# A fused attention and two-MoE kernel: a tile's value product moved in front of the next tile's scores

## Chip, cores, metric

The kernel runs on one core of one Trainium2 chip. The metric is the device time of one execution in microseconds (us). The times given are the median and the ends of several runs, and the rows below come from one more execution, taken by the hardware profiler.

## What is computed

Attention over pooled keys and values, then a dense feed-forward layer with an ELU, then a layer with eight experts, of which each token takes one. All is float32.

```python
def _attn_ref(q, k, v):            # q, k, v: (8, 8, 576, 64)
    k_p = k.reshape(B, H, 72, 8, D).mean(axis=3)
    v_p = v.reshape(B, H, 72, 8, D).mean(axis=3)
    attn = softmax(np.matmul(q, k_p.transpose(0, 1, 3, 2)) / np.sqrt(D))
    return np.matmul(attn, v_p)

x = attn_out.transpose(0, 2, 1, 3).reshape(4608, 512)
h = x @ w_in                       # (512, 2048)
g = np.where(h > 0, h, np.exp(np.minimum(h, 0)) - 1)
x = g @ w_out                      # (2048, 512)
logits = x @ w_gate                # (512, 8): one expert per token
for e in range(8):                 # w1: (512, 1024), w2: (1024, 512)
    out[mask] = gate_w[mask, None] * (np.maximum(x[mask] @ w1[e], 0) @ w2[e])
```

## The kernel before, in words

The 4608 tokens are 36 tiles of 128, and three tiles make one of 12 blocks (0 to 11). The dense layer runs in 192 steps: a step takes one block and one of the 16 slices of the 2048 hidden columns. Blocks 0 and 1 share steps 0 to 31 in quarters, and block `b` from 2 on has steps `16 b` to `16 b + 15`. In a step TensorE first makes the slice's hidden values (`g1_mm`, 12 products of 128x384, L506), ScalarE (ACT) and VectorE (DVE) apply the ELU to them (`elu_a` L516 to L518, `elu_b` L523 and L524, `elu_c` L530 and L531), and TensorE multiplies the values of two steps ago with `w_out` (`g2`, 9 products of 128x512, L548). float32 products are split into three products of rounded parts (`xh`, `xl` and so on).

The attention of a block is spread over the steps of the block in front of it, and the routing of a block over the steps of the block behind it. Which operation lies in which step is written out by hand: `at(n, slot, fn, ...)` puts `fn` into a slot of step `n`, and `step(n)` runs the slots in a fixed order. `pe_mid` lies between `g1_mm` and `g2` on TensorE, `dve_pre` in front of the ELU, `act_mid` behind `elu_b`, `end` at the end of the step. Each engine works through its own queue in that order, and so do the DMA queues of SP and of POOL (GpSimd).

For a tile `t` from 9 on: `s_mm` (L410) makes the scores of 8 heads on quarters of the array, into two PSUM banks; `s_max`, `s_exp` and `s_norm` make probabilities of them, `q_turn` (L446) turns these on VectorE in blocks of 32, and `q_move` (L454) copies the pieces into `aT`, half of the copies on ACT and half on VectorE, in two parts. `pv_mm` (L479) multiplies `aT` with the values, and `pv_copy` (L492, L493) writes the result as `xh` and `xl`, the input of the dense layer. If the scores are in step `n`, the turn is at the end of `n + 1`, the two moves are in `n + 2` and `n + 3`, and the value product is in `n + 4`. The scores of the three tiles of a block lie in steps 0, 5 and 10 of the block in front of it. The turned pieces, `aT` and the wide tile of probabilities (`s_wide`) have one buffer each, and scores, value products and counts go round three PSUM banks.

With the scores go, at a fixed distance: the load of q (`a_load`, on SP), eight transfers that sum up k and v of a batch (`k_link`, `v_link`; the first on SP, seven accumulating ones on POOL), and the scaling of k (`k_scale`). The routing of a block has 24 logits on VectorE (L599), then `r_top`, `r_weight`, and `r_count` (L662, L663), which counts the tokens' places with two small products; `r_put` works the places out on VectorE and scatters them to the list `tab` with three transfers on POOL. The last 16 steps (block 11) and all behind them belong to the experts.

Of the kernel before, what the change touches and what calls it, by code (L numbers as in the profile page):

```python
# [25 lines left out]
NT = NTOK // P  # L26
TB = 3
NBLK = NT // TB
BT = TB * P
DFF = 2048  # L30
NF = DFF // P
# [24 lines left out]
T_TURN = 9  # L56
# [41 lines left out]
def fused_kernel(ctx: ExitStack, tc: tile.TileContext, q, k, v, w_in, w_out, w_gate, w1, w2, cst, out):  # L98
# [595 lines left out]
    def at(n, slot, fn, *args):  # L694
        events.setdefault((n, slot), []).append((fn, args))
# [3 lines left out]
    def score_at(t, n, slot="pe_mid"):  # L699
        at(n, slot, s_mm, t)  # L700
        n += slot == "pe_end"
        for hh in range(2):
            at(n, "dve_pre", s_max, t, hh)
        at(n, "act_mid", s_exp, t, 0)
        n += t not in (7, 8)
        at(n, "act_mid", s_exp, t, 1)
        at(n, "dve_mid" if t in SCORE0 else "end", s_norm, t)

    def turn_at(t, n):
        at(n + 1, "end", q_turn, t)  # L710
        for part in range(2):
            at(n + 2 + part, "act_mid", q_move, t, part)
        at(n + 4, "pe_mid", pv_mm, t)
        at(n + 4, "act_mid", pv_copy, t)

    def trans_at(t, n):
        at(n, "pe_end" if t in OUT else "pe_mid", t_mm, t)
        for hh in range(2):
            at(n, "act_end" if t in OUT else "act_mid", t_copy, t, hh, nc.scalar.copy)
        out = OUT.get(t, ((n, "pe_end"), (n + 1, "pre")))  # L720
        at(*out[0], pv_mm, t)
        at(*out[1], pv_copy, t)

    at(2 * NF - 1, "end", s_wide)
    first_of = {b: b * S // P for b in range(B)}
    SCORE = {6: (20, "pe_mid"), 7: (24, "pe_mid"), 8: (28, "pe_mid")}
    TRANS = {6: 23, 7: 26, 8: 30}
# [5 lines left out]
    for t in range(2 * TB, NT):  # L733
        if t not in SCORE:
            blk, j = divmod(t, TB)
            SCORE[t] = (NF * (blk - 1) + 5 * j, "pe_mid")
            at(SCORE[t][0] - 6, "end", a_load, t)
        else:
            at(SCORE[t][0] - 6, "end", a_load, t)
        score_at(t, *SCORE[t])  # L740
        if t >= T_TURN:
            turn_at(t, SCORE[t][0])
        else:
            trans_at(t, TRANS[t])
    for b in range(2, B):
        n0 = SCORE[first_of[b]][0]
        for j in range(POOLW):
            at(n0 - 22 + j, "end", k_link, b, j)
            at(n0 - 14 + j, "end", v_link, b, j)
        at(n0 - 2, "end", k_scale, b)  # L750
# [35 lines left out]
    for x, (w, c) in enumerate(chunks):  # L786
        n = 2 + x
# [16 lines left out]
    def route_at(blk, n0, per):  # L804
        at(n0 - 3, "end", r_gate_load, blk, 0)
        at(n0 - 2, "end", r_gate_load, blk, 1)
        at(n0 - 1, "end", r_gate_load, blk, 2)
        n = 0
        for x in range(NE * TB):
            e, j = divmod(x, TB)  # L810
            at(n0 + n, ("dve_mid", "end", "end", "end")[x - sum(per[:n])], r_logit, blk, e, j)
            if j == TB - 1 and e + 3 < NE:
                at(n0 + n, "end", r_gate_load, blk, e + 3)
            if x + 1 == sum(per[:n + 1]):
                n += 1
        n += n0
        at(n, "dve_mid", r_top, blk)
        at(n + 1, "dve_mid", r_weight, blk)
        if blk < last - 1:
            at(n + 2, "pe_mid", r_count, blk)  # L820
            at(n + 2, "end", r_put, blk)

    route_at(1, 30, [1, 2, 2, 2, 2, 3, 3, 3, 3, 3])
    route_at(0, 41, [2, 2] + [3] * 6 + [2])
    route_at(2, 3 * NF + LAG + 1, [2, 2, 2, 2, 3, 3, 3, 3, 4])
    for blk in range(3, last):
        route_at(blk, NF * (blk + 1) + LAG, [3, 2, 3, 2, 3, 2, 3, 2, 2, 2])
# [572 lines left out]
    for k in range(1, len(main)):  # L1400
        kind, prev = main[k][0], main[k - 1][0]
        for u in range(TILES[kind]):
            if kind == "T":
                n = 4 * k - 2
            elif prev == "T":
                n = 4 * k - TILES[kind] + u
            else:
                n = 4 * k - 1
# [170 lines left out]
```

## Time and profile before

| what | value |
|---|---|
| median of 3 runs | 1442.6 us (1439.48 to 1446.41) |
| the profiled execution | 1439.03 us |
| its span, first to last instruction | 1437.2 us |
| TensorE (PE) busy | 1379.6 us, 96% of the span |
| VectorE (DVE) busy | 988.5 us, 69% |
| ScalarE (ACT) busy | 773.4 us, 54% |
| GpSimd (POOL) busy | 199.3 us, 14% |
| TensorE's granted clock, mean | 0.983 of full speed |

Times in the rows are counted from the first instruction. A tile's name is the program's, with the buffer's number left out; `out<-in` says what an instruction writes and reads. Steps 32 to 175 run from 189.13 to 902.97 us of the span. The releaser that the profile names for a wait is inferred from the time at which semaphores changed; where two engines ended nearly together it can be the other one.

### The profile page before, as it was taken

The numbers are of one execution on the slowest core, as the hardware profiler recorded it, in microseconds if no ns is written. First come the engines' busy times: TensorE is split into PE (matmuls) and PEld (weight loads), VectorE is DVE, ScalarE is ACT, GpSimd is POOL, SyncE is SP. The second block draws the span as 40 slices with busy tenths as digits, with TensorE's granted clock in tenths as the row PEclk, the third lists the DMA queues.
The fourth block names the chain that finished last, engine by engine and source line by source line (L and its number), as shares of the span: only waits on it lengthen the run. The fifth ranks groups of instructions, "written<-read, shape, count | busy, mean of one in ns | idle before, by whom it ended". The sixth has DMA issues, their size and how long they took to land. (4 is left out here: it accounts for less than half of the span.)

```text
span 1437.2 us, 23781 instructions
## 1 busy us (share of the span) xinstructions
PE 1379.6 (96%) x8481; PEld 1176.2 (82%) x8482; DVE 988.5 (69%) x2395; ACT 773.4 (54%) x1889; POOL 199.3 (14%) x208
## 2 busy tenths in 40 slices
PE   8999999999999999999999999999999999999996
PEld 5798888878888888888888888998888888778785
DVE  7899878887777868686868778795646544335261
ACT  6777756565666656666656566462333233334251
POOL 0011011111111211110210000020212122112020
PEclk9999999999999999999999999999999999999999
DMA  9166435556333372554461331356476447758460
GB/s 341 59 183 196 115 83 88 68 70 93 56 69 64 70 74 57 65 78 62 87 79 41 60 34 51 60 166 128 154 113 174 132 148 244 253 190 312 148 227 22
DMA packets 109144, 169.43 MB, mean 118 GB/s; under 512 B 15509, under 2 KB 53015, under 8 KB 109016
## 3 DMA queue, kind: packets, MB, share of 16 engines
q1 hardware_dynamic: 91528, 135.45, 38.6%
q0 software_dynamic: 17488, 32.37, 10.8%
q8 instruction: 69, 1.13, 0.4%
q14 instruction: 59, 0.48, 0.2%
HBM read 146.35 MB, written 21.88 MB: 117 GB/s over the span
## 5 line engine op out<-in xcount | busy, mean ns | idle before, releaser
L548 PE MATMUL y<-woh,gh 128*128 128x512 f32 x576 | 238.2, 414 | 2.0 <-DVE yr L562 2.0
L548 PE MATMUL y<-wol,gh 128*128 128x512 f32 x576 | 232.2, 403 | 0.0
L548 PE MATMUL y<-woh,gl 128*128 128x512 f32 x576 | 231.2, 401 | 0.0
L599 DVE SCALAR_TENSOR_TENSOR junk<-yr,wgb 128x512 bf16<-128x512 f32 x264 | 180.8, 685 | 4.4 <-ACT yr L564 1.3
L523 DVE SCALAR_TENSOR_TENSOR g<-g,th 128x384 f32<-128x384 f32 x192 | 106.4, 554 | 101.7 <-ACT th L518 101.0
L530 ACT CAST gh<-g 128x384 fp32r<-128x384 f32 x192 | 98.8, 515 | 136.0 <-DVE g L524 86.9
L506 PE MATMUL h<-xh,wih 128*128 128x384 f32 x768 | 168.3, 340 | 1.5 <-ACT xh L492 1.5
L506 PE MATMUL h<-xl,wih 128*128 128x384 f32 x768 | 166.5, 338 | 0.0
L506 PE MATMUL h<-xh,wil 128*128 128x384 f32 x768 | 165.9, 337 | 0.0
L516 ACT ACTIVATE th<-h 128x384 f32<-128x384 f32 x192 | 94.0, 490 | 131.8 <-PE h L506 131.7
L1222 DVE SCALAR_TENSOR_TENSOR hlD<-mhD,hhD 128x512 fp32r<-128x512 f32 x64 | 44.2, 691 | 161.3 <-ACT hhD L1221 155.9
L506 PEld LDWEIGHTS h<-xh,wih 128*128 128x128 f32 x768 | 139.7, 190 | 18.1 <-ACT xh L492 2.0
L1221 ACT ACTIVATE hhD<-mhD 128x512 fp32r<-128x512 f32 x64 | 38.4, 601 | 199.2 <-PE myD L1244 191.6
L531 DVE TENSOR_TENSOR gl<-g,gh 128x384 fp32r<-128x384 f32 x192 | 106.9, 557 | 44.9 <-ACT gh L530 39.2
L506 PEld LDWEIGHTS h<-xh,wil 128*128 128x128 f32 x768 | 137.7, 188 | 0.0
L506 PEld LDWEIGHTS h<-xl,wih 128*128 128x128 f32 x768 | 137.4, 188 | 0.2
L548 PEld LDWEIGHTS y<-woh,gh 128*128 128x128 f32 x576 | 111.2, 193 | 27.6 <-issue 7.2
L548 PEld LDWEIGHTS y<-woh,gl 128*128 128x128 f32 x576 | 111.8, 194 | 25.6
L548 PEld LDWEIGHTS y<-wol,gh 128*128 128x128 f32 x576 | 111.6, 194 | 17.5
L524 DVE TENSOR_TENSOR g<-g,h 128x384 f32<-128x384 f32 x192 | 106.3, 554 | 6.6
L518 ACT ACTIVATE th<-th 128x384 f32<-128x384 f32 x192 | 100.8, 525 | 6.2
L517 ACT ACTIVATE g<-th 128x384 f32<-128x384 f32 x192 | 100.8, 525 | 6.2
(282 smaller groups left out, 2350.3 us busy)
## 6 DMA issues: line engine op xcount, KB each, us to landing
wgb<-in_moe_w_gate_dram SPq DMA_DIRECT2D x96, 256.0 KB, 4.5
w1stD<-in_moe_w_dram SPq DMA_DIRECT2D x32, 512.0 KB, 4.4
w2stD<-in_moe_w_dram SPq DMA_DIRECT2D x32, 512.0 KB, 4.6
qT<-in_q_dram SPq DMA_DIRECT2D x36, 256.0 KB, 8.8
ybuf<-yr SPq DMA_DIRECT2D x33, 256.5 KB, 7.6
raw<-in_moe_w_in_dram SPq DMA_DIRECT2D x16, 512.0 KB, 7.6
raw<-in_moe_w_out_dram SPq DMA_DIRECT2D x15, 512.0 KB, 6.2
t1U<-in_moe_w_dram SPq DMA_DIRECT2D x12, 512.0 KB, 8.5
```

Source lines behind the costliest of these rows:

```text
L506: mark["g1"] = nc.tensor.matmul(ps, wi[i][a][:, c, o:o + P], bb[blk][:, c, :], start=n == 0, stop=n == 3 * KC - 1).ins
L516: nc.scalar.activation(th, hps[blk, f], AF.Relu, scale=-1.0)
L517: nc.scalar.activation(g, th, AF.Exp, scale=-1.0)
L518: nc.scalar.activation(th, th, AF.Tanh, scale=-0.5)
L523: nc.vector.scalar_tensor_tensor(g, g, 1.0, th, op0=ALU.add, op1=ALU.mult)
L524: nc.vector.tensor_max(g, g, hps.pop((blk, f)))
L530: nc.scalar.copy(gh, g)
L531: nc.vector.tensor_sub(gl, g, gh)
L548: nc.tensor.matmul(ys[blk][j], a[:, js], wo[i][bb][:, o, :], start=n == 0 and f in FIRST[blk], stop=n == 2 and f in LAST[blk],)
L599: nc.vector.scalar_tensor_tensor(junk, yrows[blk][j][:, :DM], 1.0, pes[blk, e], op0=ALU.mult, op1=ALU.mult, accum_out=lgs[blk][:, j, e:e + 1])
L1221: nc.scalar.activation(hh, ps, AF.Relu)
L1222: nc.vector.scalar_tensor_tensor(hl, ps, 0.0, hh, op0=ALU.max, op1=ALU.subtract)
```

## The change

The value product and its copy are taken out of `turn_at` (four steps behind the scores) and put into the step of the next tile's scores, registered in front of these; for tile 35 they stay in step 174. The scores of block 4 and later blocks lie in steps -2, 3 and 8 instead of 0, 5 and 10 of the block in front; those of tiles 9, 10 and 11 lie in steps 31, 36 and 41 instead of 32, 37 and 42. `s_wide` is made at the end of step 30 instead of 31. `r_count` and `r_put` of blocks 0 to 9 lie three steps behind `r_top` instead of two. No operation is added or left out.

```diff
@@ def turn_at(t, n)
         for part in range(2):
             at(n + 2 + part, "act_mid", q_move, t, part)
-        at(n + 4, "pe_mid", pv_mm, t)
-        at(n + 4, "act_mid", pv_copy, t)
@@
-    at(2 * NF - 1, "end", s_wide)
+    at(2 * NF - 2, "end", s_wide)
@@ for t in range(2 * TB, NT)
             blk, j = divmod(t, TB)
-            SCORE[t] = (NF * (blk - 1) + 5 * j, "pe_mid")
+            SCORE[t] = (NF * (blk - 1) + 5 * j - 2 if blk > 3 else 2 * NF - 1 + 5 * j, "pe_mid")
+            if t > T_TURN:
+                at(SCORE[t][0], "pe_mid", pv_mm, t - 1)
+                at(SCORE[t][0], "act_mid", pv_copy, t - 1)
             at(SCORE[t][0] - 6, "end", a_load, t)
@@
             trans_at(t, TRANS[t])
+    at(NF * (NBLK - 1) - 2, "pe_mid", pv_mm, NT - 1)
+    at(NF * (NBLK - 1) - 2, "act_mid", pv_copy, NT - 1)
@@ def route_at(blk, n0, per)
         if blk < last - 1:
-            at(n + 2, "pe_mid", r_count, blk)
-            at(n + 2, "end", r_put, blk)
+            at(n + 3, "pe_mid", r_count, blk)
+            at(n + 3, "end", r_put, blk)
```

## Rows read from the trace of the kernel before

**Rows 1.** Page, part 1: busy us (share of the span) and instructions of each engine.
```profile
PE 1379.6 (96%) x8481; PEld 1176.2 (82%) x8482; DVE 988.5 (69%) x2395; ACT 773.4 (54%) x1889; POOL 199.3 (14%) x208
```

**Rows 2.** TensorE's waits and their releasers: us in total, times, longest us.
```profile
PE pv L479 <- ACT th L516: 30.5, 22, 2.8
PE pv L479 <- DVE aT L454: 5.9, 5, 2.0
PE y L548 <- DVE yr L562: 2.0, 1, 2.0
PE pos L663 <- DVE acc L652: 1.6, 8, 0.2
```

**Rows 3.** Timeline, steps 115 and 116: start, length, engine, line, operation [idle before].
```profile
607.88 0.55 DVE L523 SCALAR_TENSOR_TENSOR g<-g,th 128x384 f32<-128x384 f32 x1
...
609.05 0.93 DVE L454 COPY aT<-turned 32x256 f32<-32x256 f32 x3
...
609.52 0.48 ACT L516 ACTIVATE th<-h 128x384 f32<-128x384 f32 x1
...
610.12 1.09 PE L479 MATMUL pv<-aT,v 72*64 72x128 f32 x16 [1.26 <-ACT th L516]
...
611.15 0.50 PE L548 MATMUL y<-woh,gh 128*128 128x512 f32 x1
```

**Rows 4.** Timeline, step 41.
```profile
237.33 1.09 PE L479 MATMUL pv<-aT,v 72*64 72x128 f32 x16 [1.83 <-DVE aT L454]
...
238.40 0.48 ACT L516 ACTIVATE th<-h 128x384 f32<-128x384 f32 x1
```

**Rows 5.** Windows, 27 steps with value product: length, busy us per engine, PEclk, DMA.
```profile
206.66:215.77 9.11, 7.03 (x38) 5.75 (x37) 8.66 (x24) 5.22 (x12) 0.44 (x1) 0.81 0.34 76
...
866.06:872.50 6.44, 5.48 (x39) 4.64 (x37) 6.25 (x19) 4.27 (x9) 0.00 (x0) 1.00 0.14 43
890.07:898.79 8.72, 7.12 (x40) 5.84 (x39) 6.11 (x21) 5.09 (x12) 0.00 (x0) 0.80 0.41 98
sum 202.12, PE 163.74 PEld 136.36 DVE 176.04 ACT 121.74 POOL 22.23; mean PE 6.06 PEld 5.05 DVE 6.52 ACT 4.51 POOL 0.82
```

**Rows 6.** Windows, sums over 27 steps with scores, then 90 with neither.
```profile
sum 136.10, PE 136.10 PEld 116.89 DVE 110.12 ACT 82.52 POOL 11.29; mean PE 5.04 PEld 4.33 DVE 4.08 ACT 3.06 POOL 0.42
...
sum 375.62, PE 375.62 PEld 341.28 DVE 272.17 ACT 238.47 POOL 55.70; mean PE 4.17 PEld 3.79 DVE 3.02 ACT 2.65 POOL 0.62
```

**Rows 7.** Windows of steps 29 and 31, a value product without a wait.
```profile
173.31:178.69 5.38, 5.38 (x40) 4.56 (x38) 3.45 (x8) 3.58 (x14) 0.00 (x0) 1.00 0.05 14
183.62:189.13 5.51, 5.51 (x41) 4.70 (x38) 3.07 (x8) 3.52 (x8) 1.70 (x3) 1.00 0.22 30
```

**Rows 8.** Timeline of TensorE in the prologue.
```profile
22.07 1.10 PE L479 MATMUL pv<-aT,v 72*64 72x128 f32 x16
23.09 0.73 PE L410 MATMUL sp<-kT,qT 64*64 64x72 f32 x32
23.75 1.09 PE L479 MATMUL pv<-aT,v 72*64 72x128 f32 x16
```

**Rows 9.** Windows of steps 42 and 78: counts behind scores, behind a value product.
```profile
240.53:245.63 5.10, 5.10 (x56) 4.38 (x55) 4.83 (x21) 2.10 (x5) 0.00 (x0) 1.00 0.63 145
...
419.59:426.95 7.36, 5.75 (x41) 4.75 (x39) 6.01 (x21) 5.10 (x12) 0.00 (x0) 1.00 0.17 61
```

**Rows 10.** Windows of blocks 2, 3 and 7: length, busy us of PE, PEld, DVE, ACT, POOL.
```profile
189.13:271.26 82.13, 76.24 (x484) 66.94 (x482) 70.01 (x193) 48.38 (x134) 11.67 (x13) 0.96 0.48 71
271.26:353.75 82.49, 76.70 (x501) 67.33 (x500) 67.74 (x198) 49.47 (x137) 10.49 (x12) 0.96 0.58 81
...
589.08:666.54 77.46, 73.56 (x484) 64.92 (x482) 60.12 (x163) 49.29 (x136) 11.61 (x13) 1.00 0.50 70
```

**Rows 11.** Timeline: ELU of step 119, first product of step 121.
```profile
628.76 0.55 DVE L524 TENSOR_TENSOR g<-g,h 128x384 f32<-128x384 f32 x1
...
630.89 0.87 PE L506 MATMUL h<-xh,wih 128*128 128x384 f32 x4
```

**Rows 12.** Window from step 176 to the end.
```profile
902.97:1437.20 534.23, 522.41 (x2759) 432.32 (x2757) 270.63 (x572) 193.99 (x301) 94.57 (x88) 0.99 0.56 166
```

## The prediction

> **What bounds the kernel now.** I read the page's engine line first: TensorE is busy in 1379.6 of 1437.2 us [rows 1], so 57.6 us of the span are TensorE idle time, and no other engine is near its limit as a whole. What can be won is idle time of TensorE, or busy time in which it runs slowly. The list of TensorE's waits says where the idle time lies: in front of the value product `pv` of a tile there are 30.5 + 5.9 us, and the next entry is a single wait of 2.0 [rows 2].
>
> The timeline of one such step shows what the wait is for [rows 3]. TensorE ends the first product of step 116 and stands still for 1.26 us, until `pv` starts at 610.12. The list names ACT's `th` (it ends at 610.00) as the releaser, but `pv` does not read `th`. It reads `aT`, and VectorE's last copy into `aT` (L454) ends at 609.98. In step 41 the two can be told apart: there `pv` starts behind the copy, and `th` only starts 1.07 us after `pv` has [rows 4]. So it is a wait for the move of the turned probabilities. That copy is late for a plain reason: in VectorE's queue it stands behind the two ELU operations of its step (L523 at 607.88), which need ACT's `tanh` of a product that TensorE ended a step earlier. With the value product four steps behind the scores, TensorE gets there 1 to 2 us too soon every time.
>
> The windows over whole steps give the size. The 27 steps with a value product take 202.12 us, TensorE is busy in 163.74 of them, so 38.4 are idle. Nine of the 27 show a granted clock of 0.80 to 0.84 instead of 1.00, the first and the last of them in the rows [rows 5]: the clock fell to its lower level (1.2 instead of 2.4 GHz) behind the pause. These two last 9.11 and 8.72 us, a step with a short pause and no fall 6.44. The 27 steps with scores take 136.10 us with no idle time, and the 90 steps with neither take 375.62, which is 4.174 each [rows 6]. Together, steps 32 to 175 are 713.84 us.
>
> **The change part by part.** *Value product.* Of tiles 9 to 34 it moves to the step of the next tile's scores, directly in front of them: five steps behind its own scores (six between blocks) instead of four. Tile 35 stays six behind. The copies gain a plain step of 4.17 us and were late by 1 to 2. So some 2 to 3 us are left over in an ordinary block, the wait should go, and with it the pauses behind which the clock fell. A value product without a wait is in the trace twice, in steps of 5.38 and 5.51 us [rows 7]: 1.21 and 1.34 over a plain step. I take 1.28.
>
> *The pair.* Scores alone cost 136.10 / 27 - 4.174 = 0.87 [rows 6]. Side by side they cost less: in the prologue, scores start 1.02 us behind the start of a value product, and the next value product 0.66 behind the scores, with no pause [rows 8]. The full-array product also starts 1.03 behind a value product (610.12 to 611.15 in [rows 3]), so scores put between the two add 0.66, not 0.87. A pair: 1.28 + 0.66 = 1.94.
> The Trainium skill's page "TensorEngine Tiling (Array Packing)", section Tiling Modes, says that a change of the tiling mode drains TensorE; `pv` (72*64) and the scores (64*64) are different tilings, so by that page the pair would still pay a drain in its middle. Estimated at half of the 0.21 that lone scores pay for two changes, this would be 2.04 for a pair, 2.6 us more for 26 of them. The prologue's rows show no such extra between the two, so they decide.
>
> *Scores* move two steps sooner (tiles 9 to 11: one), and with them the loads of q (SP), the links of k and v (the first on SP, seven accumulating transfers on POOL), the scaling of k (VectorE) and the strip of zeros (POOL). I cost these at nothing: they keep their distance to the scores, no wait for q or k is in the list, whose largest entries stand in [rows 2], and the buffers that they refill are released sooner by as many steps. If that cover were gone, a late q or k would stop TensorE for as long as it is late, once per tile or batch.
>
> *Counts.* The two small products of `r_count` move one step on. Today they cost 0.06 where they lie behind scores (5.10 against the mean of 5.04), and 0.30 of busy time where they lie behind a value product (5.75 - 4.174 - 1.28), with a wait for `acc` of 0.2 on top [rows 2, 9]. A step later `acc` is long done. I take 0.3 for each of ten. Their scatters (three on POOL each) come a step later, in front of links that have 14 steps in hand. VectorE's five short operations behind the counts now follow the norm and turn of the next block's first tile. The lists still read `acc` two steps after the last of them.
>
> *What is late next: VectorE.* Its work does not shrink, while TensorE's time does. At the new prices a block takes 16 x 4.174 + 3 x 1.94 + 0.3 = 72.9 us. VectorE is busy 60.1 in an ordinary block, but 70.0 in block 2 and 67.7 in block 3, where earlier blocks are routed as well [rows 10]. In an ordinary block 12.8 us are left; its tightest place is the first product that reuses the bank which the ELU reads: it starts 1.58 us behind the ELU (629.31 to 630.89) [rows 11], and by the order of the queues I find about that much after the change. In blocks 2 and 3 VectorE would have to work 96% and 93% of the time, though each tile's scores hold it up. There TensorE will have to wait for VectorE: for a bank, or for the copy of y (one wait of 2.0 us in [rows 2]; the second half of a move now lies in that copy's step). The trace of before does not show how long. From below it is 0. From above, blocks 2 and 3 keep the 82.1 and 82.5 us that they have, which gives back 19 us. I take 5, nearer the low end, since most of the 12 and 15 us that VectorE idles in them today comes with TensorE's own pauses.
>
> *The sum.* Steps 32 to 175 after: 144 x 4.174 = 601.0; 26 pairs 50.4; the value product of tile 35 1.3; the scores of tile 9, which now join a value product in step 31, 0.7; ten counts 3.0; VectorE 5.0. That is 661.4, so 52.4 less than 713.8. Behind step 175 TensorE is busy in 522.4 of 534.2 us [rows 12] and does the same as now, only sooner. The profiled execution took 1439.03 us (its span of 1437.2 and 1.8 around it): 1439.03 - 52.4 = 1386.6, say 1387. The median of the three runs is 3.6 above that execution. I don't add this: two or three more clock falls are as much, and the falls should go. It stays in the range.
>
> **The rivals.**
> *VectorE bounds the routing blocks.* 19 us instead of 5: 1401. For it: 70.0 of 72.9. Against: it is only two blocks, and the bank has 1.58 in hand. Chance 0.10.
> *The clock still falls.* If the chip takes two small products in a row, 1.9 us on a part of the array, as it takes a pause, the clock falls in a third of the pairs, as now in nine of 27. A fall costs about 1.4 us (8.72 against 7.36 for steps with the same work [rows 5, 9]), nine of them some 13: 1400. Against it: in step 169 a pause of 0.96 and a value product of 1.09, two microseconds with less work than a pair has, left the clock at 1.00 [rows 5]. Chance 0.08.
> *The wait moves along.* The value product waits for something that comes later, too, say a bank of the same step, and the pauses stay: about 1439. That in step 41 it starts right behind the copy speaks against it. Chance 0.02.
> *Slower.* TensorE works in order, so a value product that waits now holds up the scores behind it. Their maxima stand in VectorE's queue in front of the ELU and of the next copies, so lateness feeds on itself. To end above 1446, each of 26 pairs would need a wait of (52 + 7) / 26 = 2.3 us, that is copies about 5 us later against TensorE's steps than today. That needs VectorE without spare time in ordinary blocks, and it has 12.8 us. It would be some 1450. Chance 0.03.
>
> **How the numbers follow.** The forecast has 0.77, and 1376 to 1396 is its own range: no loss to VectorE and shorter pairs at the low end, 10 us of loss, a drain per pair and the 3.6 of the median at the high end. The range that should hold the time 8 times in 10 goes on to the first two rivals: 1374 to 1403. About 0.5%, 7 us, is what a measurement of this kernel can tell from no change. Faster by more: the forecast and the first two rivals, 0.95; the same 0.02; slower 0.03.
>
> **What would show it.** Right: no `pv` wait of tens of us in TensorE's list; `pv` and `sp` back to back, with starts 1.0 apart; steps with a pair of about 6.1 us; no or nearly no clock falls between 200 and 850 us; ordinary blocks of about 73 us. New in the list would be waits of `h` or `y` for VectorE, in blocks 2 and 3 above all, some 5 us together. Wrong: `pv` still waits behind the last copy; `sp` starts more than 1.2 behind `pv`; clock falls inside pairs; or ordinary blocks that keep 77 us, with waits for VectorE in them.

## The result and the profile after

| | before | after |
|---|---|---|
| median | 1442.07 us (1439.48 to 1446.41, 4 runs) | 1384.34 us (1382.43 to 1385.67, 4 runs) |
| ratio | | 0.9606, 95% interval 0.9582 to 0.9629 |
| profiled execution | 1439.03 us, span 1437.2 | 1385.67 us, span 1383.8 |
| steps 32 to 175 | 713.84 us | 659.89 us |
| from step 176 on | 534.2 us | 534.6 us |

The kernel is 57.7 us faster by the medians and 53.4 by the profiled executions; in these all of it lies in steps 32 to 175. The engine line of the page answers to [rows 1]: TensorE is idle for 26 us of the span where it was for 58.

```profile
PE 1357.7 (98%) x8481; PEld 1164.8 (84%) x8482; DVE 983.7 (71%) x2395; ACT 772.1 (56%) x1889; POOL 199.2 (14%) x208
```

The list of TensorE's waits (us in total, times, longest us) answers to [rows 2]. No tile from 9 on waits for its value product any more, and the counts don't wait. The first line is the old wait in step 22. The others are new; they name the copies of y's rows or, with `part`, the addition of block 0's parts to them.

```profile
PE y L548 <- DVE yr L562: 2.3, 1, 2.3
PE y L548 <- ACT yr L564: 1.6, 1, 1.6
...
PE y L548 <- DVE part L588: 1.4, 1, 1.4
...
PE y L548 <- DVE yr L566: 1.2, 1, 1.2
```

The timeline of steps 114 and 115 is the counterpart of [rows 3] for the first tile of an ordinary block (tile 24). VectorE's last copy into `aT` ends at 569.78, the value product starts at 574.25, 4.5 us later and without a pause. The scores of the next tile start 1.02 behind it, the full-array product 0.67 behind these, as in the prologue of the kernel before [rows 8].

```profile
568.89 0.89 DVE L454 COPY aT<-turned 32x256 f32<-32x256 f32 x3
...
574.25 1.09 PE L479 MATMUL pv<-aT,v 72*64 72x128 f32 x16
...
575.27 0.73 PE L410 MATMUL sp<-kT,qT 64*64 64x72 f32 x32
...
575.94 0.50 PE L548 MATMUL y<-woh,gh 128*128 128x512 f32 x1
```

The windows answer to [rows 5, 6, 9]: the sum over the 26 steps with a pair (a value product directly in front of the next tile's scores), over the ten steps with counts, and over the 107 steps with neither; then steps 34, 50 and 174 (the value product of tile 35), one by one (length, busy us of each engine, PEclk, DMA).

```profile
sum 158.93, PE 158.93 PEld 136.28 DVE 139.13 ACT 95.56 POOL 19.24; mean PE 6.11 PEld 5.24 DVE 5.35 ACT 3.68 POOL 0.74
...
sum 43.50, PE 43.50 PEld 37.92 DVE 20.69 ACT 26.82 POOL 0.83; mean PE 4.35 PEld 3.79 DVE 2.07 ACT 2.68 POOL 0.08
...
sum 452.07, PE 447.94 PEld 405.41 DVE 388.98 ACT 315.59 POOL 68.36; mean PE 4.19 PEld 3.79 DVE 3.64 ACT 2.95 POOL 0.64
...
197.69:203.48 5.79, 4.43 (x22) 3.75 (x21) 5.66 (x15) 4.06 (x10) 1.73 (x2) 1.00 0.23 31
271.99:280.03 8.04, 5.27 (x22) 4.06 (x22) 7.81 (x23) 6.08 (x13) 0.00 (x0) 0.92 0.55 38
839.50:844.89 5.39, 5.39 (x38) 4.58 (x37) 4.26 (x17) 2.56 (x6) 0.00 (x0) 1.00 0.67 148
```

Busy time equals length in the steps with pairs and counts. The 4.1 us by which 452.07 exceeds 447.94 are TensorE's only idle time between steps 32 and 175: 1.36 in step 34 and 2.77 in step 50. Behind the second the clock falls, once; step 51, a pair of 7.05 us, carries the rest of it. Blocks 2, 3 and 7 answer to [rows 10]:

```profile
189.31:263.61 74.30, 72.94 (x483) 64.88 (x482) 68.01 (x189) 47.51 (x134) 11.75 (x13) 1.00 0.51 89
263.61:341.47 77.86, 75.09 (x501) 66.06 (x500) 68.29 (x197) 50.34 (x143) 9.23 (x9) 0.98 0.55 72
559.56:632.29 72.73, 72.73 (x484) 64.86 (x483) 59.84 (x163) 49.21 (x137) 9.02 (x10) 1.00 0.50 71
```

The ordinary block is TensorE's work and nothing else. Blocks 2 and 3 keep 1.6 and 5.1 us more than it.

### The profile page after: what moved, and what is told of

Its sections match the earlier page's. It is cut to its first block, busy times and chain, and to the rows that moved or that the text cites. A ratio compares the mean times of both kernels' runs of the same rounds, so it can differ in the third digit from the quotient of the medians.

```text
span 1383.8 us, 23759 instructions
## 1 busy us (share of the span) xinstructions
PE 1357.7 (98%) x8481; PEld 1164.8 (84%) x8482; DVE 983.7 (71%) x2395; ACT 772.1 (56%) x1889; POOL 199.2 (14%) x208
## 4 chain that ended last, share of the span: by engine, by line
PE 85%; DVE 5%; issue 5%; ACT 3%; DMA 1%; POOL 0%; SPq 0%; POOLq 0%; ACTq 0%; DVEq 0%
PE h L506 25%; PE y L548 25%; PE mhD L1212 13%; PE myD L1247 13%; PE pv L479 2%; PE sp L410 1%; PE zTD L1142 1%; DVE dec L227 1%; DVE dec L231 1%; ACT gh L530 1%; DVE junk L599 1%; PE mhT L1212 1%; ACT dec L220 1%; PE vsum L345 1%; DVE dec L225 1%
## 5 line engine op out<-in xcount | busy, mean ns | idle before, releaser
L548 PE MATMUL y<-woh,gh 128*128 128x512 f32 x576 | 230.6, 400 | 6.4 <-DVE yr L562 2.3
L548 PE MATMUL y<-wol,gh 128*128 128x512 f32 x576 | 226.6, 393 | 0.0
L548 PE MATMUL y<-woh,gl 128*128 128x512 f32 x576 | 226.5, 393 | 0.0
L1224 ACT ACTIVATE hhD<-mhD 128x512 fp32r<-128x512 f32 x64 | 38.4, 601 | 199.3 <-PE myD L1247 183.9
L548 PEld LDWEIGHTS y<-woh,gh 128*128 128x128 f32 x576 | 108.1, 188 | 28.0 <-issue 2.8
L548 PEld LDWEIGHTS y<-woh,gl 128*128 128x128 f32 x576 | 108.3, 188 | 24.0
L548 PEld LDWEIGHTS y<-wol,gh 128*128 128x128 f32 x576 | 108.3, 188 | 16.2
```

Source lines behind the costliest of these rows:

```text
L548: nc.tensor.matmul(ys[blk][j], a[:, js], wo[i][bb][:, o, :], start=n == 0 and f in FIRST[blk], stop=n == 2 and f in LAST[blk],)
```

## The experiments

Three questions: is the wait of the value product really one for the copies into `aT`; which part of the change carries how much; and is VectorE what holds up blocks 2 and 3 now. The theory is that of the prediction. Its rivals were that `pv` waits for ACT's `th`, that the sooner scores and not the later value product bring the gain, and that pairs or the place of the counts are worth nothing.

**e1: value products four steps behind their scores again, all else changed.**

```diff
-                at(SCORE[t][0], "pe_mid", pv_mm, t - 1)
+        at(n + 4, "pe_mid", pv_mm, t)      # in turn_at; pv_copy alike
```


> The changed kernel with one part undone: the value product of tiles 9 to 35 is four steps behind its own scores again, in a step of its own; scores stay sooner, counts stay later. Theory (the gain is the wait for the move of aT, and the clock falls behind it): the waits come back, TensorE's list shows some 27 waits of pv of 1 to 2 us, 25 to 40 us in all, clock falls come back (3 to 12 of them), pairs are gone; 1425 to 1445 us. Rival (the gain comes from VectorE's work lying better once the scores are sooner): at most 1395 us, with few pv waits.

1407.5 us (1403.6 to 1409.1; ratio to before 0.9746, 0.9715 to 0.9776). Neither had it: the later value product (with the pairs) brings 23 of the 58 us, sooner scores and later counts together bring 35. How these 35 divide was not run on its own; e9 below shows the counts alone to be worth 2 us or nothing. TensorE's waits for the value product, by who ended them:

```profile
PE pv L479 <- ACT th L516: 12.1, 9, 1.8
PE pv L479 <- DVE aT L454: 4.9, 11, 0.9
```

The windows of steps 114, 119 and 124 (first, second and third tile of a block; columns as above):

```profile
583.23:588.62 5.39, 5.39 (x39) 4.58 (x37) 4.18 (x10) 4.56 (x10) 0.00 (x0) 1.00 0.04 3
606.14:612.64 6.50, 5.47 (x38) 4.62 (x37) 6.31 (x19) 4.28 (x10) 0.62 (x1) 1.00 0.59 109
630.22:635.93 5.71, 5.48 (x39) 4.63 (x37) 5.55 (x15) 3.56 (x8) 0.87 (x1) 1.00 0.24 36
```

Waits come back, but 17 us in all instead of 38, and three clock falls instead of nine. So it matters which steps of a block the moves lie in. The first tile's are now in steps 0 and 1, which have no logits, instead of 2 and 3, which have three and two, and four steps are enough (no idle time, 1.26 us before). The second tile's lie among two or three logits as before, and it waits 1.03 us (0.96 before). The third tile's left steps 12 and 13, and its wait falls from 1.4 to 0.23 us. That is not a matter of logits: those two steps have none, but `r_top` and `r_weight`. In the first of them ACT stood 2.58 us until VectorE had made `lg`, and what ACT had queued behind that came late, as this line of the kernel before shows (step 124, for the value product of step 126):

```profile
654.25 0.22 ACT L627 ACTIVATE lg<-lg 128x24 f32<-128x24 f32 x1 [2.58 <-DVE lg L626]
```

Which of the operations in front of the moves costs how much, no run separates.

**e3 and e8: the kernel before, with the moves in front of the ELU instead of behind it; e8 also has the counts one step later.**

```diff
-            at(n + 2 + part, "act_mid", q_move, t, part)
+            at(n + 2 + part, "dve_pre", q_move, t, part)
 # e8 also:
-            at(n + 2, "pe_mid", r_count, blk)          # r_put alike
+            at(n + 3, "pe_mid", r_count, blk)
```


> The kernel before with one edit: the moves into aT stand in front of the ELU of their step (slot dve_pre) instead of behind it; the value product stays four steps behind the scores. Theory (pv waits for VectorE's last copy, which stands behind the ELU): the pv waits fall from 36 us to under 5, the clock falls with them from nine to at most two, 1385 to 1400 us. Rival (pv waits for ACT's th, the releaser that the list names): th moves no sooner, the pv waits stay at 30 us or more, 1435 to 1446 us.

e3 takes 1450.7 us (1448.0 to 1454.2; ratio 1.006, 1.004 to 1.008): 0.6% slower, above the ranges of both. But the waits of `pv` fell, from 36.4 us to 12.1 (not to under 5: the first tile of a block still waits 1.2 us), so they do follow the copies. The time was lost in other waits, of TensorE for the counts above all, and of the hidden-value products `h` for the ELU, which now stands behind the copies:

```profile
PE pos L662 <- DVE roh L650: 22.2, 10, 2.5
PE pv L479 <- ACT th L518: 9.3, 8, 1.2
PE h L506 <- DVE g L524: 5.7, 10, 3.0
...
PE pv L479 <- DVE aT L454: 2.3, 5, 0.9
```

The counts of step 14 need `roh`, which VectorE makes behind the ELU of the step in front; the wait of `pv` had covered that. With that cover gone the pause moves from in front of the value product to behind it, gets longer (2.5 instead of 1.4 us), and the clock still falls behind it. e8 moves the counts away from there:

> The kernel before with the moves in front of the ELU (as in e3) and the counts one step later: that step no longer has a value product, so that a late r_weight stops nothing. Theory (pv waits for the copies; in e3 the time was lost again at the counts): waits of pos for roh gone, pv waits about 11 us as in e3, few clock falls; 1400 to 1415 us, some 30 us under the kernel before. Rival (moves in front of the ELU cost as much as they save, whatever the counts do): 1435 us or more.

1408.1 us (1407.7 to 1409.0; ratio 0.9771, 0.9736 to 0.9806), as the theory had it. The waits of `pv` are 13.0 us, and no clock fall is left between steps 32 and 175: its list of waits, then the window over these steps:

```profile
PE pv L479 <- ACT th L518: 9.4, 8, 1.2
PE h L506 <- DVE g L524: 3.4, 10, 1.1
PE pv L479 <- DVE aT L454: 3.0, 6, 1.3
...
188.44:870.79 682.35, 663.35 (x4389) 582.04 (x4388) 556.26 (x1515) 444.48 (x1223) 87.76 (x96) 1.00 0.45 70
```

So the order of one kind of copies and the place of two small products are worth 33 us together, with scores and value products where they were. That `pv` waits for the copies is shown; the releaser in the list was an accident of two ends lying together. The trace of the kernel before also shows for which half of them: in 24 of its 27 steps `pv` starts 0.10 to 0.25 us behind the end of VectorE's last copy, while ACT's last copy had ended 0.98 to 2.45 us before that start. (The other three tiles span two batches; there `pv` starts 0.2 us before VectorE's last copy ends.) ACT's last copies for the value product of [rows 3] end at 607.87, 2.25 us before it starts:

```profile
606.64 1.23 ACT L454 COPY aT<-turned 32x256 f32<-32x256 f32 x3
```

**e9: the kernel before, counts one step later, nothing else.**

> The kernel before with one part of the change alone: the counts one step later. Theory (this part is worth its wait for acc, 0.3 us each, and fewer clock falls in step 14, whose stretch of pause and small products becomes shorter by 0.6 us; four or five of the nine falls are there): pv waits as before, 36 us, two to five falls less, 1428 to 1437 us. Rival (it changes nothing alone): 1438 to 1444 us.

1439.4 us (1433.0 to 1441.9, 10 runs; ratio 0.9985, 0.9964 to 1.0006). Waits of `pv` are as before (37.2 us), and the clock falls eight times instead of nine, where the theory had two to five falls less. A gain of 2 us by the medians, which the interval does not tell from none; it lies in the rival's range. The later counts pay only together with another part: behind e3's copies they are worth some 42 us (e8 against e3).

**e4: the changed kernel, counts two steps behind `r_top` again.**

> The changed kernel with one part undone: the counts (and the places) lie two steps behind r_top again, which for eight blocks is the step of a pair. Theory: scores, value products and counts go round three banks, so the count then needs the bank of the value product two products in front of it, and waits for VectorE's copy out of it, about 2.4 us; 8 x 2.4 = 19 us more, about 1403, with waits of pos for DVE xl in TensorE's list. Rival (the step of the counts does not matter, 0.3 us each in either place): 1384 us.

1412.0 us (1407.3 to 1419.0; ratio 0.9802, 0.9765 to 0.9839), 28 more than the changed kernel and 9 above the theory's 1403. The wait is there, 19.9 us in seven steps (the eighth, step 174, has no scores and no wait), and so is one clock fall more, in block 3. In the profiled executions, 21.6 us apart, this is nearly all; why the runs of e4 spread upwards from there by 12 us is not shown. Its line in TensorE's list of waits:

```profile
PE pos L662 <- DVE xl L493: 19.9, 7, 4.4
```

The timeline of step 110, the count with its wait in brackets:

```profile
564.73 0.73 PE L410 MATMUL sp<-kT,qT 64*64 64x72 f32 x32
...
567.31 0.68 DVE L493 TENSOR_TENSOR xl<-pv,xh 128x512 fp32r<-128x512 f32 x1
...
568.05 0.19 PE L662 MATMUL pos<-roh,tri 128*128 128x24 bf16 x1 [2.58 <-DVE xl L493]
```

Value product, scores (two banks) and count are four takers of three banks in one step. The count gets the bank of the value product and stands until VectorE has copied it, behind maxima and ELU.

**e5: the changed kernel, scores of block 4 and later in steps 0, 5 and 10 again.** The value product of a block's third tile must be ready before the block begins, so it stays in step 14, four behind its scores and alone.

```diff
-            SCORE[t] = (NF * (blk - 1) + 5 * j - 2 if blk > 3 else 2 * NF - 1 + 5 * j, "pe_mid")
+            SCORE[t] = (NF * (blk - 1) + 5 * j if blk > 3 else 2 * NF - 1 + 5 * j, "pe_mid")
...
+            if t % TB == 0 and t > T_TURN:
+                at(SCORE[t][0] - 2, "pe_mid", pv_mm, t - 1)      # pv_copy alike
```


> The changed kernel with one part undone: scores of block 4 and later lie in steps 0, 5 and 10 of the block in front again. The value products of a block's first two tiles stand in front of the next tile's scores as in the changed kernel; that of the third must be made before the block begins and lies in step 14, four behind its scores, alone. Theory (four steps are too few wherever steps with logits lie between): eight waits of pv of some 1.4 us are back (11 us), with two to five clock falls of 1.4 and eight pairs less at 0.2: 1395 to 1405 us. Rival (the place of the scores is free, only pairs and distance of the first two tiles count): 1384 to 1388 us.

1408.5 us (1407.7 to 1410.2; ratio 0.9776, 0.9745 to 0.9806), just above the range of the theory. TensorE's list of waits:

```profile
PE pv L479 <- ACT th L516: 12.6, 8, 2.9
PE pos L662 <- DVE xl L493: 5.1, 1, 5.1
```

The window of step 53:

```profile
283.81:297.09 13.28, 8.13 (x73) 6.70 (x71) 9.41 (x32) 5.13 (x17) 0.68 (x1) 0.82 1.00 111
```

The eight third tiles wait 12.6 us, as expected. What I had overlooked is that the scores of tile 13 now meet a count in step 53, the collision of e4: that step is 7.2 us longer than a pair (13.28 against 6.07). Without it the time would lie at about 1401, by subtraction. So the sooner scores are what lets the third tile be six steps behind. They also have a price that this run shows: here step 50 has no wait, so the wait there in the changed kernel came with the sooner scores of block 4.

**e2: value products late, but apart from the scores.**

```diff
+        late = n + (5 if t % TB == 2 else 6)
+        at(late, "pe_mid", pv_mm, t)       # pv_copy alike; one pair is left, tile 11 with 12's scores
```


> The changed kernel with the value product late enough but not beside scores: six steps behind its own scores for the first two tiles of a block (one step behind the next tile's scores), five for the third. One pair is left (tile 11 with the scores of tile 12). Theory (a pair saves the 0.21 us that lone scores pay for entering and leaving their tiling): no pv waits, 25 x 0.21 = 5 us more than the changed kernel, about 1389.5 us. Rival, by the page on tilings (a drain in the middle of a pair is paid as well): half of that, about 1387. Second rival (neighbourhood is worth nothing): 1384.

1386.4 us (1385.1 to 1390.9; ratio 0.9619, 0.9587 to 0.9651). No `pv` wait. By its time alone the run decides nothing: it lies nearest to the rival with the drain (1387), and within 2.1 us of the changed kernel in both sets of its runs (1384.3, and 1386.0 in e0 below). The windows decide. Sums of the windows over 26 steps with a value product, and over 25 with scores:

```profile
sum 140.47, PE 140.47 PEld 119.81 DVE 102.03 ACT 92.03 POOL 18.33; mean PE 5.40 PEld 4.61 DVE 3.92 ACT 3.54 POOL 0.70
...
sum 125.71, PE 125.71 PEld 107.93 DVE 114.76 ACT 73.19 POOL 14.87; mean PE 5.03 PEld 4.32 DVE 4.59 ACT 2.93 POOL 0.59
```

Apart they cost 1.229 + 0.854 = 2.08 over plain steps, together 1.90, so a pair saves 0.18 of TensorE's time: the 0.21 of the prologue's rows, and not the half of it that a drain in the middle would leave. Yet 25 such savings, 4.5 us, show in the time as 0.4 to 2.1 us. e10 looks for the rest.

**e6: scores first, value product behind them.** The same pair, the registration of `pv_mm` and `pv_copy` moved behind `score_at`.

> The changed kernel with the two halves of a pair in the other order: the next tile's scores first, then the value product. VectorE gets the scores 1.0 us sooner in 26 steps and stands still less before the maxima. Theory (VectorE is what is late in blocks 2 and 3, held up by the scores): the waits of y for yr and part there, some 4 us and a clock fall, shrink by half or more; 1380 to 1383 us. Rival (the order is free, VectorE has its time elsewhere): 1384 us, the same waits.

1385.9 us (1384.7 to 1386.8), the changed kernel on the same chip (e0 below) 1386.0 (1384.2 to 1386.5). The rival is right: the waits of y are the same to 0.1 us, and the order within the pair is free in time.

**e7: the copies into `aT` of tiles 9 to 14 all on ACT.**

```diff
-            copy = (nc.scalar.copy, nc.vector.tensor_copy)[i % 2]
+            copy = (nc.scalar.copy, nc.vector.tensor_copy)[i % 2 if t > 14 else 0]
```


> The changed kernel, but all copies into aT of tiles 9 to 14 are made by ACT: VectorE has 0.9 us less work in each of twelve steps of blocks 2 and 3, ACT 1.2 us more. Theory (VectorE's load in the routing blocks costs what TensorE still waits there): the waits of y in steps 34 and 50 (4 us) and the clock fall behind the second go, 1377 to 1381 us. Rival (ACT, which also copies y, becomes late instead): the waits of y stay and name ACT, 1384 us or more.

1379.6 us (1379.3 to 1381.6; ratio 0.9577, 0.9552 to 0.9602), 6.4 less than the changed kernel beside it, with no overlap of the runs; it is the fastest version here. The windows of steps 34 and 50, and of blocks 2 and 3:

```profile
196.47:201.24 4.77, 4.44 (x22) 3.75 (x21) 4.74 (x12) 4.58 (x12) 0.86 (x1) 1.00 0.42 57
269.75:275.63 5.88, 4.46 (x22) 3.75 (x21) 4.33 (x12) 5.67 (x13) 0.00 (x0) 1.00 0.59 22
188.10:261.38 73.28, 72.95 (x484) 64.87 (x483) 64.21 (x175) 55.52 (x155) 11.74 (x13) 1.00 0.56 93
261.38:335.74 74.36, 72.94 (x502) 64.82 (x501) 61.92 (x175) 56.57 (x158) 9.42 (x9) 1.00 0.58 71
```

The idle time in the two steps falls from 4.1 to 1.75 us, and no clock fall is left there. So VectorE's load was the cause of 2.4 of the 4.1 us and of the fall. What stays is mostly in step 50 (1.4 us) and names ACT, which copies two of y's three rows: the rival has a part of it.

**e0: the changed kernel again, beside e5, e6 and e7.**

> The changed kernel once more, beside the others on the same chip, for differences of less than 0.5%: 1382 to 1386 us.

1386.0 us (1384.2 to 1386.5), at the top of what was expected; its steps 34 and 50 wait as in the first run.

**e10: e2 with ACT's copies of e7, and e7 again beside it.**

> e2 (value products apart from scores) with the copies of tiles 9 to 14 on ACT as in e7, beside e7 itself. Theory (a pair saves 0.18 us of TensorE in every block, but in the changed kernel blocks 2 and 3 give it back as waits for VectorE; with VectorE relieved it shows in full): 25 x 0.18 = 4.5 us more than e7, some 1384 us. Rival (a pair saves nothing in time): within 1.5 us of e7.

> The kernel of e7 once more, on the same chip as e10, for a difference of less than 0.5%: 1379 to 1381 us.

e10 1384.2 us (1383.7 to 1386.0), e7 again 1382.0 (1380.5 to 1383.0), 1 us above what was expected of it. The window over steps 32 to 175 of e10:

```profile
189.31:849.23 659.92, 658.07 (x4358) 579.82 (x4356) 543.81 (x1478) 455.55 (x1251) 88.30 (x95) 1.00 0.48 72
```

The same window of e7 again:

```profile
187.60:842.73 655.13, 653.40 (x4358) 582.04 (x4356) 543.46 (x1478) 455.12 (x1251) 88.27 (x95) 1.00 0.49 73
```

In this stretch pairs save 4.8 us, as the theory says; the same windows of e2 and e0 differ by 0.1 us (661.11 and 661.18). There the changed kernel gives the saving back in block 3, which takes 77.76 us in e0 and 75.81 in e2: with pairs the wait in step 50 is longer (2.8 against 2.1 us), and the clock falls behind it, which it does not in e2. In the medians e10 and e7 differ by 2.1 us, which lies between the 4.5 of the theory and the 1.5 of the rival; e7's own medians in two sets of runs lie 2.4 apart. So the saving of a pair is shown on TensorE, and its size in the time is open: 0.4 to 2.1 us in the changed kernel, 2 to 5 with VectorE relieved.

## Why the prediction was right, and where its steps were not

*The wait and its cause.* Right. The 38.4 us of idle time are down to 4.1, and e3 and e8 show the copies as the cause, VectorE's half of them by the trace. The nine clock falls went with the pauses, but for one behind the new pause in step 50. The idle time is 34 of the 54 us; pairs are some 5, and most of the other 15 is the clock.

*Scores sooner at nothing.* The sum stands, the costing does not. I took the sooner scores for a free companion of the move, but e1 shows that together with the counts they do more than half of the work, and e5 that the third tile needs them. I had counted only the distance in steps, not what VectorE and ACT have to do in the steps of the moves. The trace after has both: in ordinary blocks the second tile's copies are 3.1 to 3.3 us ahead, about the step of 4.17 less the 0.96 that they were late, but the first tile's are 4.5 ahead where 2.9 would follow, and the third's 7.9 to 8.2 where two steps would give 6.9.

*The pair.* 1.94 predicted, 1.90 measured ((158.93 - 7.05) / 25 - 4.174, without the step that carries the clock fall). The Trainium skill's page "TensorEngine Tiling (Array Packing)", section Tiling Modes, says that a change of mode drains TensorE; it gives no price, and the estimate of half of 0.21 for it would have made a pair 2.04. The windows after and those of e2 decide for the rows. No further extra for the change from `pv` to the scores can be seen: scores follow a value product after 1.02 us, the full-array product followed it after 1.03.

*Counts.* 0.3 each predicted, 0.18 measured (43.50 / 10 - 4.174). The reason was incomplete: I moved them out of the way of a wait of 0.2 for `acc`. What the place really avoids is a wait of 2.6 us for a bank (e4). In that the later counts were lucky: no term of the prediction had it, and the kernel before could not show it, as scores and counts met there only in step 42, with no value product beside them.

*VectorE.* 5 us predicted, 6.5 measured: 452.07 - 107 x 4.174 = 5.5, and 1.0 in step 51. Right in the stretch and, for the larger part, in the engine (e7; 1.4 us stay and name ACT). Of the two places that I named, the bank that the ELU reads does not stop TensorE; the copy of y does, in step 34, where block 0's parts are added, and in step 50.

*The sum.* 661.4 us for steps 32 to 175, measured 659.9; 1386.6 for the execution, the profiled one took 1385.67. One of its terms, 0.7 for the scores of tile 9, is a cost of step 31 (5.51 us before, 6.15 after), which lies in front of that stretch; without it the stretch has 660.7. That the sum is so close is in part luck: pairs, tile 35 and counts were taken 2.3 us too dear, VectorE 1.5 too cheap. Leaving the 3.6 us of the median out came out right: before, the median lay above the profiled execution, and after it lies 1.3 below it. With four runs of each, where the profiled one falls among them is chance.

*The rivals.* VectorE as the bound of blocks 2 and 3 is real, at 6.5 us and not 19. No clock fall begins in a pair: 25 of the 26 windows have a granted clock of 1.00, and the one of step 51 has its fall from step 50. The wait did not move along in the changed kernel, but it did in e3 and, as a wait for a bank, in e4 and e5, each time to the counts. The slower rival had no ground: the copies are 3.1 us or more ahead in all ordinary blocks.

## What to carry to other kernels

When an engine that works in order stands still in front of the same operation in every round, because what it reads is not ready, give that operation one more step. But look first at what else the engines that make its input have queued in those steps: moving that, and two small products, brought 33 us here (e8) with the operation where it was; the whole change brought 58. Before an operation is moved into a step, count the takers of every small ring of buffers there; a count of 0.2 us stood for 2.6 because it was the fourth taker of three banks. And after the bound engine has been sped up, add up the next one's load block by block: here two of nine blocks gave back 6.5 us, more than the pairs save in all of them.

## What was not expected of the hardware

A pause moved is not a pause of the same price. The windows over steps 32 to 175 of the kernel before and of e3:

```profile
189.13:902.97 713.84, 675.46 (x4390) 594.52 (x4388) 558.33 (x1521) 442.73 (x1223) 89.21 (x97) 0.98 0.44 67
...
187.10:913.06 725.96, 683.12 (x4390) 598.05 (x4388) 558.15 (x1521) 446.03 (x1223) 88.35 (x97) 0.97 0.43 66
```

In e3 the pauses were little longer in sum (42.8 against 38.4 us), but the longest stood behind the value product, in front of the counts. The clock fell ten times, once more than before, and TensorE was busy for 683.1 us with the work that had taken 675.5. So of the 12.1 us by which this stretch grew, 4.4 are pauses and 7.7 are work that ran slower.

And a pause of 1.36 us left TensorE's clock at 1.00 in one block, and in the next it fell behind a pause of 1.35, as these windows of e5 show (the same step of blocks 4 and 5):

```profile
410.81:417.65 6.84, 5.48 (x38) 4.64 (x37) 5.50 (x21) 5.07 (x11) 0.00 (x0) 1.00 0.12 39
...
485.17:493.54 8.37, 7.02 (x39) 5.72 (x38) 6.11 (x21) 5.25 (x12) 1.65 (x2) 0.80 0.51 111
```

That may be why runs of a kernel with such pauses can lie far apart (1436.0 to 1447.8 for the kernel before over all its runs, 1407.3 to 1419.0 for e4). It is not shown: e5, whose clock fell five times, spread by 2.5 us only.
